# A gated mix of linear attention and an MLP on one core: three groups of products split into 64-row halves, and the blocks' order rewritten

## The chip, the cores and the metric

One core of one Trainium2 chip. The kernel is launched once per run; the time of a run is the device time in microseconds (us). The kernel before was run three times: 446.23, 444.49 and 444.58 us, median 444.58. A profile of one execution on the chip gives the durations of single instructions. TensorE (PE in the profile) multiplies, with a separate instruction that loads the stationary operand (PEld); VectorE is DVE, ScalarE is ACT, GpSimd is POOL, and SyncE (SP) issues most DMAs.

## The reference

```python
x = A_x                                   # 1 x 2048 x 512
g = sigmoid((x * gate_w).sum(-1, keepdims=True))
# A: linear attention, 32 heads of 16
q, k, v = split(x @ wqkv)
phi(u) = concat(softmax(u @ w_phi), softmax(-(u @ w_phi)))
o = phi(q) @ (phi(k).T @ v) / (phi(q) @ phi(k).T @ 1 + 1e-6)
a = o.reshape(B, S, D) @ wo               # wo: 512 x 512
# B: dense, mish, dense
h = x @ w1 + b1                           # w1: 512 x 1376
b = (h * tanh(softplus(h))) @ w2          # w2: 1376 x 512
out = g * a + (1 - g) * b
```

## The kernel before, in words

*Precision.* The large products are done in fp32r, a type of four bytes that TensorE takes in one pass. Each operand X is split into a part h rounded to fp32r and a rest l = X - h, and a product of two operands becomes three: h with h, h with l, l with h.

*Stages.* Stage A goes over the 2048 rows in eight pieces of 256 and makes k, v, q and phi(k); it sums phi(k).T v and phi(k).T 1 in PSUM and SBUF. The change leaves it alone. Stage B goes over four blocks of 512 rows, B0 to B3. A block has eleven hidden groups of 128 (`ORDER`), and for each group i:

- `up` (L516): 12 products of 128 contraction rows into one PSUM bank: w1 (h) with x (h), w1 (l) with x (h), w1 (h) with x (l), four pieces of the contraction each. The bank holds 128 hidden columns of 512 rows.
- `mi` (L527, ScalarE): mish from that bank into SBUF, which frees the bank. `hi` (L532, ScalarE) makes h, `lo` (L540, GpSimd) makes l. Group 0 has an odd number of rows and needs a second `hi` and a part of `lo` on ScalarE; `gr` reads its gate row from the same bank.
- `down` (L559; steps `dn0` to `dn9`, and `df0` to `df3` for the last group): h and l as stationary operands against w2, for four row tiles t: three products each, 12 in all (8 for group 0), summed into four banks, one for each t, over the whole block. `fi` (VectorE) joins a finished bank with the attention part and stores it.

Attention in a block: `nu` (num) multiplies phi(q) by the sums in 64-row, 32-column pieces of the array, `oh` (ScalarE) and `ol` (VectorE) split the result, `wo_` (L676) multiplies by wo in 12 products per row tile, and `ag` (ScalarE) scales it out of its bank. `cd` adds what is left of group 0 in four 32-row pieces. While a block's products run, VectorE and ScalarE make phi(q) of the next one (`mx`, `mn`, `d0`, `d1`, `E`, `S`, `T`, `D`, ..., `es`, `tr`).

*PSUM.* Eight banks: three called "a" (`up`, half of `nu`, `wo`), four called "dn" (the sums of `down`), one called "kv" (`nu`, and `wo` for even t). A bank goes to the next user in turn, once the last one's reader is done.

*Order.* Nothing is planned by a program: the texts `BLOCK0` (B0), `BLOCK1` (B1) and `BLOCK` (B2 and B3; L62 to L84) list the steps, `run` (L201) issues them in that order, and `pin` keeps each engine in the order of issue. A "+" means the next block's step. Every product goes through `mm` (L100), so the profile gives L101 for all of them; ScalarE's steps go through `act` (L121).

Of the kernel before, what the change touches and what calls it, by code (L numbers as in the profile page):

```python
# [59 lines left out]


BLOCK0 = """  # L62
    up0 lq3 mi0 gr hi0 lo0 ldo0 ldo1 S1 rS1 up1 up2 mi1 hi1 lo1 wh0 wl0 d02 d12 T0 D0 m0 de0 rd0 sc0 es0 tr0 mi2 hi2 up3 dn0 hc lo2
    mi3 hi3 lo3 T1 D1 m1 de1 rd1 sc1 es1 tr1 mv0 lq0+ lq1+ mx3 mn3 d03 d13 WH0 dn1
    up4 mi4 hi4 lo4 WH1 WL0 dn2 E2 S2 T2 rS2 D2 m2 de2 rd2 sc2 es2 tr2 up5 mi5 hi5 lo5 WL1 dn3 E3 ge gg up6 mi6 hi6 lo6 dn4
    up7 mi7 hi7 lo7 dn5 S3 T3 rS3 D3 m3 de3 rd3 sc3 es3 tr3 mv1 up8 mi8 hi8 lo8 dn6
    mx0+ mn0+ d00+ d10+ mx1+ mn1+ d01+ d11+ lq2+ lq3+ up9 mi9 hi9 lo9 dn7 E0+ E1+ S0+ T0+ LX0 rS0+ D0+ m0+ de0+ rd0+ sc0+
    up10 mi10 hi10 lo10 dn8 dn9 cd nu0 nu1 oh0 ol0 es0+ tr0+ XH0+ XL0+ S1+ T1+ rS1+ LX1 df0 df1 wo0 ag0 wo1 oh1 ol1 ag1 D1+ fi0
    m1+ de1+ rd1+ sc1+ df2 df3 wo2 ag2 fi1 XH1+ XL1+ es1+ fi2 wo3 ag3 fi3 tr1+ mv0+
"""  # L70
BLOCK1 = """
    up0 mi0 hi0 lo0 gr mx2 mn2 d02 d12 mx3 mn3 d03 d13 up1 mi1 hi1 lo1 lq0+ lq1+ E2 E3 hc S2 T2 rS2 D2 m2 de2 rd2 sc2 es2 tr2
    up2 mi2 hi2 lo2 dn0 S3 T3 rS3 D3 m3 de3 rd3 sc3 es3 tr3 mv1 up3 mi3 hi3 lo3 dn1 up4 mi4 hi4 lo4 dn2
    mx0+ mn0+ d00+ d10+ mx1+ mn1+ d01+ d11+ lq2+ lq3+ up5 mi5 hi5 lo5 dn3 E0+ E1+ ge gg
    S0+ T0+ rS0+ D0+ m0+ de0+ rd0+ sc0+ es0+ tr0+ up6 mi6 hi6 lo6 dn4 up7 mi7 hi7 lo7 dn5 cd nu0 nu1 oh0 ol0 S1+ T1+ rS1+ D1+ LX0 LX1
    m1+ de1+ rd1+ sc1+ es1+ dn6 wo0 ag0 wo1 ag1 oh1 ol1 tr1+ mv0+ dn7 up8 mi8 hi8 lo8 mx2+ mn2+ d02+ d12+ mx3+ mn3+ d03+ d13+
    wo2 ag2 up9 mi9 hi9 lo9 dn8 E2+ E3+ up10 mi10 hi10 lo10 wo3 ag3 XH0+ XL0+ XH1+ XL1+ dn9 df0 fi0 df1 fi1 df2 fi2 df3 fi3
"""
BLOCK = """
    up0 mi0 hi0 lo0 gr lq0+ lq1+ S2 T2 rS2 D2 m2 de2 rd2 sc2 es2 tr2 up1 mi1 hi1 lo1 hc up2 mi2 hi2 lo2 dn0  # L80
    S3 T3 rS3 D3 m3 de3 rd3 sc3 es3 tr3 mv1 up3 mi3 hi3 lo3 dn1 up4 mi4 hi4 lo4 dn2
    mx0+ mn0+ d00+ d10+ mx1+ mn1+ d01+ d11+ lq2+ lq3+ up5 mi5 hi5 lo5 dn3 E0+ E1+ ge gg
    S0+ T0+ rS0+ D0+ m0+ de0+ rd0+ sc0+ up6 mi6 hi6 lo6 dn4 cd nu0 nu1 oh0 ol0 es0+ tr0+ S1+ T1+ rS1+ D1+ LX0 LX1 m1+ de1+ rd1+ sc1+
    es1+ dn5 wo0 ag0 wo1 ag1 oh1 ol1 tr1+ mv0+ dn6 up7 mi7 hi7 lo7 wo2 ag2 mx2+ mn2+ d02+ d12+ mx3+ mn3+ d03+ d13+  # L84
    up8 mi8 hi8 lo8 dn7 E2+ E3+ up9 mi9 hi9 lo9 wo3 ag3 up10 mi10 hi10 lo10 dn8 XH0+ XL0+ XH1+ XL1+ dn9 df0 fi0 df1 fi1 df2 fi2 df3 fi3
"""


@with_exitstack
def tile_gated_mix(ctx: ExitStack, tc: tile.TileContext, xT, wv, wkT, wqT, bd, w1a, w1b, b1, w2a, w2b, wo, out):  # L90
# [6 lines left out]
    pin = tc.keep_in_program_order  # L97
    V, G_, A_, Sy = nc.vector, nc.gpsimd, nc.scalar, nc.sync

    def mm(*a, **k):  # L100
        return pin(nc.tensor.matmul(*a, **k))  # L101
# [410 lines left out]
    def b_ops(b):  # L512
        key = ("B", b)
        U, dn, eTs, num, ohl, io, ed = {}, {}, {}, {}, {}, {}, {}

# [159 lines left out]
        for t in range(4):  # L675
            def wo_(t=t):  # L676
                num["wo", t] = ps = psum("wo", ("kv", "a")[t % 2])
                woh, wol = [kt(wob[x], 512) for x in "hl"]

                todo = [(G, a, w) for G in range(NG) for a, w in ((0, woh), (0, wol), (1, woh))]  # L680
                if t % 2 == 0:
                    todo.sort(key=lambda x: x[1])
                for n, (G, a, w) in enumerate(todo):
                    o = a * 512 + (G % 2) * SC + (t % 2) * P
                    mm(ps, ohl[t // 2, G // 2][:, o : o + P], w[:, G, :], start=(n == 0), stop=(n == 3 * NG - 1))

            def ag(t=t):
                i = 4 * b + t
                io[t] = k2("io", "io")
                act(io[t], num["wo", t], scale=g_sb[:, i : i + 1])  # L690

            def most():

                i = S // P - 1
                pin(V.scalar_tensor_tensor(io[3], dn[3], og_sb[:, i : i + 1], io[3], op0=ALU.mult, op1=ALU.add))

            def rest():

                i = S // P - 1
                for j, eng in enumerate((Sy, A_)):  # L700
                    cs = slice(256 * j, 256 * j + 256)
# [7 lines left out]
                    pin(V.scalar_tensor_tensor(io[3][:, cs], ps, og_sb[:, i : i + 1], io[3][:, cs], op0=ALU.mult, op1=ALU.add))  # L709
# [182 lines left out]
```

## Time and profile before

| | us |
|---|---|
| median of three runs | 444.58 |
| the runs | 444.49 to 446.23 |
| span of the profiled execution (its own time outside the profiler isn't given) | 442.5 |
| TensorE busy | 437.8 |
| VectorE busy | 313.2 |
| ScalarE busy | 201.4 |
| GpSimd busy | 159.6 |
| weight loads busy (under the products) | 359.9 |

How to read it: the span runs from the first to the last instruction of one execution. Products overlap in the array, so one's duration (0.389 us for 512 columns) is longer than the distance from one start to the next; it is the distance that counts. A row of the timeline gives the start, the length, the engine, the line, the tile written and the tiles read, the rows and columns of the array in use (128*128), the shape of the moving operand and the number of instructions that were merged.

### The profile page before, as it was taken

The page shows a single profiled execution, that of the slowest core. Times are in us where ns is not written, and L with a number is a line of the kernel's source. Part 1 is how long each engine was busy: PE and PEld are TensorE (multiplying, and loading weights), DVE is VectorE, ACT ScalarE, POOL GpSimd, SP SyncE. Part 2 cuts the span into 40 slices and gives each one's busy share as a digit, 9 for nine tenths or more (in the row PEclk, how much of TensorE's full clock was granted, in tenths as well). Part 3 has the DMA queues.
Part 4 walks back from the last instruction along what each step waited for, and adds up shares of the span by engine and source line. Part 5 has one row for each costly group of instructions (what it writes and reads, how often), then busy time and mean ns, then how long its engine had stood idle before and what let it go on. Part 6 is the DMA issues. An engine that isn't in the chain of part 4 may idle for free.

```text
span 442.5 us, 7179 instructions
## 1 busy us (share of the span) xinstructions
PE 437.8 (99%) x2874; PEld 359.9 (81%) x2874; DVE 313.2 (71%) x420; ACT 201.4 (46%) x286; POOL 159.6 (36%) x100
## 2 busy tenths in 40 slices
PE   8999999999999999999999999999999999999996
PEld 7888888888888888887888878888878888887885
DVE  3987739559699999999999898279679329601103
ACT  3644523533345455736376533646352645341330
POOL 3078694785662453621024120215310222411121
PEclk9999999999999999999999999999999999999999
DMA  7721631524403136425362533222605302310002
GB/s 265 283 96 48 191 120 50 188 86 133 167 29 116 49 84 209 142 101 168 128 205 96 159 124 120 75 96 95 191 0 192 94 2 96 134 57 1 0 0 96
DMA packets 29001, 49.64 MB, mean 112 GB/s; under 512 B 6308, under 2 KB 15012, under 8 KB 28968
## 3 DMA queue, kind: packets, MB, share of 16 engines
q1 hardware_dynamic: 28648, 48.79, 32.9%
q8 instruction: 22, 0.36, 0.3%
q10 hardware_dynamic: 288, 0.39, 0.3%
q14 instruction: 11, 0.09, 0.1%
q0 software_dynamic: 32, 0.01, 0.0%
HBM read 31.73 MB, written 16.79 MB: 110 GB/s over the span
## 4 chain that ended last, share of the span: by engine, by line
PE 98%; DMA 1%; SPq 0%; DVE 0%; issue 0%
PE proj L101 30%; PE up L101 27%; PE down L101 27%; PE wo L101 10%; PE kvp L101 2%; PE num L101 2%; DMA wT<-in_wkT_dram 1%; PE fuse L101 1%; PE rest L101 0%; DVE io L709 0%; SPq L157 0%; SPq L149 0%
## 5 line engine op out<-in xcount | busy, mean ns | idle before, releaser
L543 POOL TENSOR_TENSOR l<-act,h 128x512 fp32r<-128x512 f32 (+1 forms) x44 | 62.6, 1425 | 215.5 <-ACT h L121 192.7
L121 ACT ACTIVATE act<-up,b1s 128x512 f32<-128x512 f32 x44 | 30.3, 688 | 83.1 <-PE up L101 81.0
L330 POOL TENSOR_TENSOR zacc<-zacc,E 128x1024 f32<-128x1024 f32 x16 | 39.7, 2479 | 39.9 <-DVE E L287 31.4
L121 ACT ACTIVATE E<-E 128x1024 f32<-128x1024 f32 x32 | 33.5, 1060 | 36.0 <-DVE E L272 35.9
L287 DVE TENSOR_TENSOR E<-E,Sm 128x1024 f32<-128x1024 f32 x32 | 45.1, 1409 | 1.0
L101 PE MATMUL wo<-woh,ohl 128*128 128x512 f32 x128 | 41.2, 389 | 0.0
L276 DVE TENSOR_REDUCE Sm<-E 128x64 f32<-128x1024 f32 x32 | 38.5, 1204 | 0.0
L101 PE MATMUL down<-w2ah,h 128*128 128x512 f32 x96 | 37.6, 392 | 0.0
L101 PE MATMUL down<-w2al,h 128*128 128x512 f32 x80 | 31.2, 390 | 0.0
L101 PE MATMUL down<-w2ah,l 128*128 128x512 f32 x80 | 31.1, 389 | 0.0
L121 ACT ACTIVATE h<-act 128x512 fp32r<-128x512 f32 (+2 forms) x48 | 30.3, 632 | 1.6
L101 PE MATMUL down<-w2bh,h 128*128 128x512 f32 x78 | 30.6, 392 | 0.0
L101 PE MATMUL down<-w2bl,h 128*128 128x512 f32 x78 | 30.4, 389 | 0.0
L101 PE MATMUL down<-w2bh,l 128*128 128x512 f32 x78 | 30.4, 389 | 0.0
L431 DVE TENSOR_TENSOR xbl<-xraw,xbh 128x1024 fp32r<-128x1024 f32 x8 | 10.9, 1378 | 27.1 <-ACT xbh L121 27.1
L256 DVE TENSOR_REDUCE mx<-proj 128x32 f32<-128x512 f32 x16 | 11.0, 689 | 25.5 <-PE proj L101 25.5
L101 PEld LDWEIGHTS wo<-woh,ohl 128*128 128x128 f32 x128 | 24.0, 188 | 5.0
L121 ACT ACTIVATE io<-wo,g_sb 128x512 f32<-128x512 f32 x16 | 11.0, 690 | 36.0 <-PE wo L101 34.7
L121 ACT ACT_TABLE_LOAD x19 | 24.4, 1283 | 3.5 <-PE up L101 3.2
L101 PE MATMUL up<-xbh,w1ah 128*128 128x512 f32 x96 | 25.8, 390 | 0.0
L101 PE MATMUL up<-xbh,w1al 128*128 128x512 f32 x96 | 25.7, 389 | 0.0
L101 PE MATMUL up<-xbl,w1ah 128*128 128x512 f32 x96 | 25.7, 389 | 0.0
(125 smaller groups left out, 978.3 us busy)
## 6 DMA issues: line engine op xcount, KB each, us to landing
ed<-E SPq DMA_DIRECT2D x16, 512.0 KB, 2.9
eT<-ed SPq DMA_DIRECT2D x64, 128.0 KB, 3.2
xraw<-in_xT_dram SPq DMA_DIRECT2D x15, 512.0 KB, 4.3
pqd<-qs SPq DMA_DIRECT2D x16, 256.0 KB, 2.1
pq<-pqd SPq DMA_DIRECT2D x16, 256.0 KB, 3.8
out_dram<-io SPq DMA_DIRECT2D x15, 256.0 KB, 2.0
raw<-in_w1a_dram SPq DMA_DIRECT2D x3, 512.0 KB, 4.6
raw<-in_w2a_dram SPq DMA_DIRECT2D x3, 512.0 KB, 3.7
```

The costliest lines, as they stand in the source:

```text
L101: return pin(nc.tensor.matmul(*a, **k))
L121: return pin(A_.activation(out_, in_, fn, **k))
L256: pin(V.tensor_reduce(d[name], hv(src()), axis=AX.X, op=op))
L276: pin(V.tensor_reduce(d["S"], hv(d["E"][:, :]), axis=AX.X, op=ALU.add))
L287: pin(eng.tensor_mul(hv(d["E"][:, :]), hv(d["E"][:, :]), d["S"][:, :, None].to_broadcast([P, 2 * H, DH])))
L330: at(key, f"z{t}", lambda d=d: pin(G_.tensor_add(zacc, zacc, d["E"])))
L431: pin(V.tensor_sub(xb[b][1][:, :, sl], kt(raw[h], SC), f32(xb[b][0][:, :, sl])))
L543: pin(G_.tensor_sub(U[i]["l"][:n, :], U[i]["a"][:n, :], f32(U[i]["h"][:n, :])))
```

## The change

Each product of `up`, `down` and `wo_` is given as two: contraction rows 0 to 63 and 64 to 127, which are different halves of the array. A new function `weave` takes the list of products of several steps and issues them in pairs. The first half goes through the list from its beginning, the second half from its middle and then around, so that the two halves of a pair write to different banks. Both halves of a product add into the same bank at different times. Where a bank goes from one half to the other, an empty instruction on TensorE waits for the last product of the other half in that bank. The steps are named in parentheses in the texts, such as `(up0|up1|up2)`: 36 products, 36 pairs.

The texts are new. `up` goes out in threes, or in twos with a `down`; `wo` in pairs or mixed with `up` and `down`. Steps of the other engines keep their places by and large; `oh1` and `ol1` come directly after `oh0` and `ol0`, and `fi` takes the order 0, 2, 1, 3. In B3 the last two groups' `down` for t = 0 to 2 and the tile `rest` stay whole. The work of the other engines is the same.

```diff
+    def weave(ops):
+        n = len(ops)
+        todo = [(r, ops[(i + r * (n // 2)) % n]) for i in range(n) for r in (0, 1)]
+        banks = [op[0].name for _, op in todo]
+        last = {b: i for i, b in enumerate(banks)}
+        for i, (r, (out_, a, w, opens, closes)) in enumerate(todo):
+            b, s = banks[i], slice(64 * r, 64 * r + 64)
+            row, ins = newest.get(b, (r, None))
+            if row != r:
+                hold = pin(nc.tensor.nop())
+                tc.add_manual_dep(hold.ins, ins, mybir.DependencyInfo(mybir.DependencyClass.Sync, mybir.DependencyReason.DATA), reason="row tiles take turns in a bank")
+            ins = mm(out_, a[s], w[s], start=opens and banks.index(b) == i, stop=closes and last[b] == i, skip_group_check=True)
+            newest[b] = r, ins.ins.name
+
+    newest = {}
...
     def run(text, key, prev=None, nxt=None, prev2=None):
         for w in text.split():
+            if w[0] == "(":
+                weave(sum([ops.pop((key, x))() for x in w[1:-1].split("|")], []))
+                continue
...
-            n = 0
-            for w, a in ((0, xh), (1, xh), (0, xl)):
-                for k in range(KT):
-                    mm(ps, w1_tile(f, w, k), a[:, k, :], start=(n == 0), stop=(n == 3 * KT - 1))
-                    n += 1
             U[i] = {"ps": ps}
+            return [(ps, w1_tile(f, w, k), a[:, k, :], True, True) for w, a in ((0, xh), (1, xh), (0, xl)) for k in range(KT)]
...
-            for n, (a, w) in enumerate(((h, w2_tile(f, 0)), (h, w2_tile(f, 1)), (l, w2_tile(f, 0))) if i else ((h, w2x["a"]), (l, w2x["b"]))):
-                mm(dn[t], a, w, start=(i == 0 and n == 0), stop=(i == (NF - 3 if t == last_t else NF - 1) and n == 2))
+            return [(dn[t], a, w, i == 0, i == (NF - 3 if t == last_t else NF - 1))
+                    for a, w in (((h, w2_tile(f, 0)), (h, w2_tile(f, 1)), (l, w2_tile(f, 0))) if i else ((h, w2x["a"]), (l, w2x["b"])))]
...
+                return [(ps, ohl[t // 2, G // 2][:, o : o + P], w[:, G, :], True, True)
+                        for a, w in ((0, woh), (0, wol), (1, woh)) for G in range(NG) for o in (a * 512 + (G % 2) * SC + (t % 2) * P,)]
```

The new texts (only the first of the old ones is shown):

```diff
 BLOCK0 = """
-    up0 lq3 mi0 gr hi0 lo0 ldo0 ldo1 S1 rS1 up1 up2 mi1 hi1 lo1 wh0 wl0 d02 d12 T0 D0 m0 de0 rd0 sc0 es0 tr0 mi2 hi2 up3 dn0 hc lo2
...
+    (up0|up1|up2) lq3 mi0 gr hi0 lo0 ldo0 ldo1 S1 rS1 mi1 hi1 lo1 wh0 wl0 d02 d12 T0 D0 m0 de0 rd0 sc0 es0 tr0 mi2 hi2 (up3|up4|dn0) hc lo2
+    mi3 hi3 lo3 T1 D1 m1 de1 rd1 sc1 es1 tr1 mv0 lq0+ lq1+ mx3 mn3 d03 d13 WH0 (dn1)
+    mi4 hi4 lo4 WH1 WL0 E2 S2 T2 rS2 D2 m2 de2 rd2 sc2 es2 tr2 (up5|up6|dn2) mi5 hi5 lo5 WL1 E3 ge gg mi6 hi6 lo6 (dn3)
+    (up7|up8|dn4) mi7 hi7 lo7 S3 T3 rS3 D3 m3 de3 rd3 sc3 es3 tr3 mv1 mi8 hi8 lo8 (dn5)
+    mx0+ mn0+ d00+ d10+ mx1+ mn1+ d01+ d11+ lq2+ lq3+ (up9|up10|dn6) mi9 hi9 lo9 E0+ E1+ S0+ T0+ LX0 rS0+ D0+ m0+ de0+ rd0+ sc0+ mi10 hi10 lo10 (dn7)
+    (dn8) cd nu0 nu1 oh0 ol0 oh1 ol1 es0+ tr0+ XH0+ XL0+ S1+ T1+ rS1+ LX1 (dn9) (wo0|wo1|df0) ag0 ag1 D1+ fi0
+    m1+ de1+ rd1+ sc1+ fi1 (wo2|wo3|df2) XH1+ XL1+ es1+ ag2 fi2 ag3 fi3 tr1+ mv0+
 """
 BLOCK1 = """
...
+    (up0|up1|up2) mi0 hi0 lo0 gr mx2 mn2 d02 d12 mx3 mn3 d03 d13 mi1 hi1 lo1 lq0+ lq1+ E2 E3 hc S2 T2 rS2 D2 m2 de2 rd2 sc2 es2 tr2
+    mi2 hi2 lo2 (dn0) S3 T3 rS3 D3 m3 de3 rd3 sc3 es3 tr3 mv1 (up3|up4|dn1) mi3 hi3 lo3 mi4 hi4 lo4
+    mx0+ mn0+ d00+ d10+ mx1+ mn1+ d01+ d11+ lq2+ lq3+ (up5|up6|dn2) mi5 hi5 lo5 E0+ E1+ ge gg
+    S0+ T0+ rS0+ D0+ m0+ de0+ rd0+ sc0+ es0+ tr0+ mi6 hi6 lo6 (dn3) (up7|up8|dn4) mi7 hi7 lo7 mi8 hi8 lo8 cd nu0 nu1 oh0 ol0 oh1 ol1 S1+ T1+ rS1+ D1+ LX0 LX1
+    m1+ de1+ rd1+ sc1+ es1+ (dn5) (wo0|wo1|dn6) ag0 ag1 tr1+ mv0+ mx2+ mn2+ d02+ d12+ mx3+ mn3+ d03+ d13+
+    (wo2|up9|dn7) ag2 mi9 hi9 lo9 E2+ E3+ (wo3|up10|dn8) ag3 mi10 hi10 lo10 XH0+ XL0+ XH1+ XL1+ (dn9) (df0|df2) fi0 fi2 fi1 fi3
 """
 BLOCK = """
...
+    (up0|up1|up2) mi0 hi0 lo0 gr lq0+ lq1+ S2 T2 rS2 D2 m2 de2 rd2 sc2 es2 tr2 mi1 hi1 lo1 hc mi2 hi2 lo2 (dn0)
+    S3 T3 rS3 D3 m3 de3 rd3 sc3 es3 tr3 mv1 (up3|up4|dn1) mi3 hi3 lo3 mi4 hi4 lo4
+    mx0+ mn0+ d00+ d10+ mx1+ mn1+ d01+ d11+ lq2+ lq3+ (up5|up6|dn2) mi5 hi5 lo5 E0+ E1+ ge gg
+    S0+ T0+ rS0+ D0+ m0+ de0+ rd0+ sc0+ mi6 hi6 lo6 (dn3) (dn4) cd nu0 nu1 oh0 ol0 oh1 ol1 es0+ tr0+ S1+ T1+ rS1+ D1+ LX0 LX1 m1+ de1+ rd1+ sc1+
+    es1+ (dn5) (wo0|wo1|dn6) ag0 ag1 tr1+ mv0+ (up7|wo2|up8) mi7 hi7 lo7 ag2 mx2+ mn2+ d02+ d12+ mx3+ mn3+ d03+ d13+
+    mi8 hi8 lo8 (dn7) E2+ E3+ (up9|wo3|up10) mi9 hi9 lo9 ag3 mi10 hi10 lo10 (dn8) XH0+ XL0+ XH1+ XL1+ END
 """
+END = "(dn9) (df0|df2) fi0 fi2 fi1 fi3", "df0 fi0 df1 fi1 df2 fi2 df3 fi3"
```

B2 ends with the first text of `END`, B3 with the second.

More of the change, by code (lines that the diff above doesn't have):

```diff
@@ L62 @@
 BLOCK0 = """
-    up0 lq3 mi0 gr hi0 lo0 ldo0 ldo1 S1 rS1 up1 up2 mi1 hi1 lo1 wh0 wl0 d02 d12 T0 D0 m0 de0 rd0 sc0 es0 tr0 mi2 hi2 up3 dn0 hc lo2
[L64 to L67, printed above, removed]
@@ L68 @@
-    up10 mi10 hi10 lo10 dn8 dn9 cd nu0 nu1 oh0 ol0 es0+ tr0+ XH0+ XL0+ S1+ T1+ rS1+ LX1 df0 df1 wo0 ag0 wo1 oh1 ol1 ag1 D1+ fi0
-    m1+ de1+ rd1+ sc1+ df2 df3 wo2 ag2 fi1 XH1+ XL1+ es1+ fi2 wo3 ag3 fi3 tr1+ mv0+
+    (up0|up1|up2) lq3 mi0 gr hi0 lo0 ldo0 ldo1 S1 rS1 mi1 hi1 lo1 wh0 wl0 d02 d12 T0 D0 m0 de0 rd0 sc0 es0 tr0 mi2 hi2 (up3|up4|dn0) hc lo2
+    mi3 hi3 lo3 T1 D1 m1 de1 rd1 sc1 es1 tr1 mv0 lq0+ lq1+ mx3 mn3 d03 d13 WH0 (dn1)
+    mi4 hi4 lo4 WH1 WL0 E2 S2 T2 rS2 D2 m2 de2 rd2 sc2 es2 tr2 (up5|up6|dn2) mi5 hi5 lo5 WL1 E3 ge gg mi6 hi6 lo6 (dn3)
@@ L70 @@
+    (up7|up8|dn4) mi7 hi7 lo7 S3 T3 rS3 D3 m3 de3 rd3 sc3 es3 tr3 mv1 mi8 hi8 lo8 (dn5)
+    mx0+ mn0+ d00+ d10+ mx1+ mn1+ d01+ d11+ lq2+ lq3+ (up9|up10|dn6) mi9 hi9 lo9 E0+ E1+ S0+ T0+ LX0 rS0+ D0+ m0+ de0+ rd0+ sc0+ mi10 hi10 lo10 (dn7)
+    (dn8) cd nu0 nu1 oh0 ol0 oh1 ol1 es0+ tr0+ XH0+ XL0+ S1+ T1+ rS1+ LX1 (dn9) (wo0|wo1|df0) ag0 ag1 D1+ fi0
+    m1+ de1+ rd1+ sc1+ fi1 (wo2|wo3|df2) XH1+ XL1+ es1+ ag2 fi2 ag3 fi3 tr1+ mv0+
 """
 BLOCK1 = """
-    up0 mi0 hi0 lo0 gr mx2 mn2 d02 d12 mx3 mn3 d03 d13 up1 mi1 hi1 lo1 lq0+ lq1+ E2 E3 hc S2 T2 rS2 D2 m2 de2 rd2 sc2 es2 tr2
@@ L73 @@
[L73 to L77, printed above, removed]
+    (up0|up1|up2) mi0 hi0 lo0 gr mx2 mn2 d02 d12 mx3 mn3 d03 d13 mi1 hi1 lo1 lq0+ lq1+ E2 E3 hc S2 T2 rS2 D2 m2 de2 rd2 sc2 es2 tr2
@@ L78 @@
 """
 BLOCK = """
[L80 to L84, printed above, removed]
@@ L85 @@
-    up8 mi8 hi8 lo8 dn7 E2+ E3+ up9 mi9 hi9 lo9 wo3 ag3 up10 mi10 hi10 lo10 dn8 XH0+ XL0+ XH1+ XL1+ dn9 df0 fi0 df1 fi1 df2 fi2 df3 fi3
+    (up0|up1|up2) mi0 hi0 lo0 gr lq0+ lq1+ S2 T2 rS2 D2 m2 de2 rd2 sc2 es2 tr2 mi1 hi1 lo1 hc mi2 hi2 lo2 (dn0)
+    S3 T3 rS3 D3 m3 de3 rd3 sc3 es3 tr3 mv1 (up3|up4|dn1) mi3 hi3 lo3 mi4 hi4 lo4
+    mx0+ mn0+ d00+ d10+ mx1+ mn1+ d01+ d11+ lq2+ lq3+ (up5|up6|dn2) mi5 hi5 lo5 E0+ E1+ ge gg
+    S0+ T0+ rS0+ D0+ m0+ de0+ rd0+ sc0+ mi6 hi6 lo6 (dn3) (dn4) cd nu0 nu1 oh0 ol0 oh1 ol1 es0+ tr0+ S1+ T1+ rS1+ D1+ LX0 LX1 m1+ de1+ rd1+ sc1+
@@ L199, in at @@
         steps.setdefault((key, name), []).append(fn)
+    ops = {}
     def run(text, key, prev=None, nxt=None, prev2=None):
         for w in text.split():
+            if w[0] == "(":
+                weave(sum([ops.pop((key, x))() for x in w[1:-1].split("|")], []))
+                continue
             k = {"'": prev, '"': prev2, "+": nxt}.get(w[-1], key)
@@ L563, in down, with last_down @@
             h, l = [U[i][x][:, t * P : (t + 1) * P] for x in "hl"]
-            for n, (a, w) in enumerate(((h, w2_tile(f, 0)), (h, w2_tile(f, 1)), (l, w2_tile(f, 0))) if i else ((h, w2x["a"]), (l, w2x["b"]))):
-                mm(dn[t], a, w, start=(i == 0 and n == 0), stop=(i == (NF - 3 if t == last_t else NF - 1) and n == 2))
-        for i in range(NF):
-            at(key, f"up{i}", lambda i=i: up(i))
+            return [(dn[t], a, w, i == 0, i == (NF - 3 if t == last_t else NF - 1))
+                    for a, w in (((h, w2_tile(f, 0)), (h, w2_tile(f, 1)), (l, w2_tile(f, 0))) if i else ((h, w2x["a"]), (l, w2x["b"])))]
+        def last_down(i, t):
+            for n, (o, a, w, _, closes) in enumerate(down(i, t)):
+                mm(o, a, w, start=False, stop=closes and n == 2, skip_group_check=True)
+        for i in range(NF):
+            ops[key, f"up{i}"] = lambda i=i: up(i)
+            if i < NF - (2 if b == NB - 1 else 1):
+                ops[key, f"dn{i}"] = lambda i=i: sum([down(i, t) for t in range(4)], [])
+            elif b < NB - 1:
+                for j in (0, 2):
+                    ops[key, f"df{j}"] = lambda i=i, j=j: down(i, j) + down(i, j + 1)
+            else:
+                for t in range(4):
+                    if t != last_t:
+                        at(key, f"df{t}", lambda i=i, t=t: last_down(i, t))
             at(key, f"mi{i}", lambda i=i: mi(i))
@@ L571, in b_ops @@
             at(key, f"lo{i}", lambda i=i: lo(i))
-            for t in range(4):
-                if t != last_t or i < NF - 2:
-                    at(key, f"dn{i}" if i < NF - (2 if b == NB - 1 else 1) else f"df{t}", lambda i=i, t=t: down(i, t))
         at(key, "hc", hc)
@@ L678, in wo_ @@
                 woh, wol = [kt(wob[x], 512) for x in "hl"]
[L680 to L685, printed above, removed]
+                return [(ps, ohl[t // 2, G // 2][:, o : o + P], w[:, G, :], True, True)
+                        for a, w in ((0, woh), (0, wol), (1, woh)) for G in range(NG) for o in (a * 512 + (G % 2) * SC + (t % 2) * P,)]
             def ag(t=t):
@@ L715, in fi @@
                 pin(Sy.dma_start(out[i * P : (i + 1) * P, :], io[t]))
-            at(key, f"wo{t}", wo_)
+            ops[key, f"wo{t}"] = wo_
             at(key, f"ag{t}", ag)
@@ L829, in tile_gated_mix @@
     for b in range(NB):
-        run((BLOCK0, BLOCK1, BLOCK, BLOCK)[b], ("B", b), ("B", b - 1), ("B", b + 1))
-    assert not steps, list(steps)
+        run((BLOCK0, BLOCK1, BLOCK.replace("END", END[0]), BLOCK.replace("END", END[1]))[b], ("B", b), ("B", b - 1), ("B", b + 1))
+    assert not steps and not ops, (list(steps), list(ops))
 _OUTS = [((S, D), 'float32')]
```

## The prediction

> **What bounds the kernel now.** I read the page first: busy time by engine, then the chain that ended last.
>
> ```profile
> PE 437.8 (99%) x2874; PEld 359.9 (81%) x2874; DVE 313.2 (71%) x420; ACT 201.4 (46%) x286; POOL 159.6 (36%) x100
> PE 98%; DMA 1%; SPq 0%; DVE 0%; issue 0%
> PE proj L101 30%; PE up L101 27%; PE down L101 27%; PE wo L101 10%; PE kvp L101 2%; PE num L101 2%; DMA wT<-in_wkT_dram 1%; PE fuse L101 1%; PE rest L101 0%; DVE io L709 0%; SPq L157 0%; SPq L149 0%
> ```
>
> TensorE is busy for 437.8 of 442.5 us and nothing makes it wait; up, down and wo, which the change touches, hold 64% of the chain. Any wait of TensorE is new time, and only shorter products win any. Next, the busy times of the four row blocks B0 to B3 (columns: stretch, length, then PE, PEld, DVE, ACT, POOL, granted clock):
>
> ```profile
> 149.28:221.82 72.54, 72.54 (x384) 59.21 (x377) 69.42 (x93) 38.49 (x53) 22.05 (x15) 1.00 0.41 132
> 221.82:294.18 72.36, 72.36 (x378) 59.12 (x376) 57.16 (x80) 38.96 (x53) 15.04 (x11) 1.00 0.35 117
> 294.18:366.58 72.40, 72.40 (x377) 59.10 (x376) 49.48 (x71) 33.58 (x48) 16.12 (x11) 1.00 0.31 103
> ```
>
> The clock is granted in full. Each block takes 72.4 us, and in B0 VectorE is busy for 69.4 of it: B0 could not lose more than 3 us whatever TensorE did. Now the pace of one product, from the chain in order of time and from the timeline:
>
> ```profile
> 294.34 8.16 PE up L101 x36
> 205.40 0.39 PE L101 MATMUL down<-w2bh,l 128*128 128x512 f32 x1
> 205.72 0.51 PE L101 MATMUL down<-w2al,hc 32*128 32x512 f32 x4
> 206.16 1.96 PE L101 MATMUL num<-eT,kvb 64*32 64x256 f32 x64
> 207.26 0.85 PE L101 MATMUL num<-eT,kvb 64*32 64x256 f32 x24
> 207.69 0.42 PE L101 MATMUL num<-eT,kvb 64*32 64x256 f32 x8
> L101 PE MATMUL num<-eT,kvb 64*32 64x256 f32 x256 | 7.8, 379 | 0.0
> 208.04 0.50 PE L101 MATMUL down<-w2bh,h 128*128 128x512 f32 x1
> 208.38 0.40 PE L101 MATMUL down<-w2bl,h 128*128 128x512 f32 x1
> 206.16 1.48 PEld L101 LDWEIGHTS num<-eT,kvb 64*32 64x32 f32 x64 [0.25 <-issue]
> 208.04 0.19 PEld L101 LDWEIGHTS down<-w2bh,h 128*128 128x128 f32 x1 [0.41 <-ACT ohl L121]
> 208.15 0.19 PEld L101 LDWEIGHTS down<-w2bl,h 128*128 128x128 f32 x1
> ```
>
> 36 products in 8.16 us are 0.2267 us each, every one with weights of its own. The array is already used in pieces here: "num" runs eight 64-row, 32-column pieces per turn, 64 of them in 1.96 us where one takes 0.38 from start to end. Its last three turns (x24) begin at 207.26, the last of them (x8) at 207.69: 0.43 for two turns, 0.215 each. So pieces do run side by side, and a turn of these costs less than 0.2267.
>
> **The change part by part.** *The halves.* In the new text I count 308 products in a block, 284 in B3 (where the last 18 stay whole): 1208 pairs of halves replace 1208 products. A pair's price isn't in the trace. Its ends are 0.215 (num's turn; 0.213 to 0.217 as the two starts are rounded to 0.01) and 0.2267 (today's product): 14 to 16.5 us won at most, 0 at least; the end above is a rival below. I take 0.2267, because the nearest row is another one: four 32-row pieces of the same type (fp32r) and width (512), in four banks at once, the row with x4. They cost 0.51 where one alone behind a switch of shape costs 0.50 (208.04), so they do run side by side. But they end no sooner than a whole product: from 205.72 to the next shape at 206.16 is 0.44; take off their spread, 0.01, and one weight load in the open, 0.11 (from 208.04 to 208.15, where the next load can start), and 0.32 is left, exactly what the 128-row product at 205.40 takes to the next shape at 205.72. For num, whose last piece starts at 207.69 + 0.42 - 0.38 = 207.73, it is 0.31 after a turn of 0.215: the emptying then takes about 0.09 in all three, and the 512 fp32r columns 0.227, whether 32 or 128 rows are at work. Num differs by its type: its tiles are plain fp32, 256 columns in two passes (the code issues 128, the trace has 256). The 0.013 belongs to the stream, by this reading, and halving the rows doesn't remove it.
>
> The Trainium skill, page "TensorE: Matmul & The Clock Gate", section "Measured speedup vs the span model", gives about 4 ns more for each further tile in the array; by it a pair would cost 0.231 and the sum would be 4.8 us higher. The x4 row agrees for a single turn (0.51 against 0.50), but num's starts are spread by 0.04 in a turn (0.42 less 0.38) and its turns still follow at 0.215, so I charge nothing for it.
>
> *The weight loads* double in number. Two 128-column loads of 0.11 fit under 0.2267 even one after the other; num's 64 loads in 1.48 us run side by side. Charged nothing; the other end is a rival below.
>
> *The holds.* An empty instruction waits wherever a bank goes over to the other half: by the new texts 362 at most. Everything on TensorE stands behind it. What it waits for lies at least three turns back (13 times three, else four or more), and a reader of a product starts 0.49 us after that product started (up's twelfth product starts at 295.99 + 1.07 - 0.39 = 296.67, its reader at 297.16, rows below), that is 2.2 turns. So the hold opens in time, and a wait already served costs nothing today: dn0 at 302.34, which waits for ScalarE and GpSimd, starts 0.23 after the up product before it. Charged 0; if each of the 13 laid a load open, 1.4 us.
>
> *The order.* This is the term that I charge. Three up groups are woven over 36 turns, 36 x 0.2267 = 8.16 us: up0's second half runs in turns 18 to 29, up1 and up2 end with the last turn. Before, up0 was ready 5.4 us ahead of dn0; now six turns, 1.36 us. Rows of B2 (ScalarE and GpSimd behind up0, TensorE beside them), of the group up7, and of B0:
>
> ```profile
> 295.99 1.07 PE L101 MATMUL up<-xbl,w1ah 128*128 128x512 f32 x4
> 301.43 1.07 PE L101 MATMUL up<-xbl,w1ah 128*128 128x512 f32 x4
> 302.34 0.39 PE L101 MATMUL down<-w2ah,h 128*128 128x512 f32 x1
> 297.16 0.69 ACT L121 ACTIVATE act<-up,b1s 128x512 f32<-128x512 f32 x1 [5.63 <-PE up L101]
> 297.88 1.29 ACT L121 ACTIVATE h<-act 96x512 fp32r<-96x512 f32 x2
> 298.65 1.29 POOL L543 TENSOR_TENSOR l<-act,h 96x512 fp32r<-96x512 f32 x1 [9.04 <-ACT h L121]
> 347.81 0.69 ACT L121 ACTIVATE act<-up,b1s 128x512 f32<-128x512 f32 x1 [2.09 <-PE up L101]
> 348.52 0.63 ACT L121 ACTIVATE h<-act 128x512 fp32r<-128x512 f32 x1
> 349.29 1.29 POOL L543 TENSOR_TENSOR l<-act,h 128x512 fp32r<-128x512 f32 x1 [4.15 <-issue]
> 345.02 0.69 ACT L121 ACTIVATE io<-wo,g_sb 128x512 f32<-128x512 f32 x1 [1.31 <-DMA eT<-ed]
> 152.33 0.69 ACT L121 ACTIVATE act<-up,b1s 128x512 f32<-128x512 f32 x1 [2.92 <-PE up L101]
> 155.63 0.69 ACT L121 ACTIVATE act<-up,b1s 128x512 f32<-128x512 f32 x1
> ```
>
> - dn0 in B1, B2, B3, alone behind (up0|up1|up2): up0's last turn starts at 29 x 0.2267 = 6.57, mi0 at 7.06, and l is there 2.78 later (297.16 to 299.94), at 9.84; with the load, 9.95. dn0 needs l in its second turn, at 8.16 + 0.23 = 8.39. Wait 1.56, three times: 4.7 us.
> - dn7 in B2 and B3, alone behind (up7|wo2|up8): mi7 at 7.06, l 2.77 later (347.81 to 350.58) and the load make 9.94; needed in the third turn, 8.61. Wait 1.33, twice: 2.7 us.
> - (up3|up4|dn0) in B0: its first turn writes up4 into up1's bank, free once mi1 has read it. mi0 at 7.06, mi1's end 3.99 later (152.33 to 156.32): 11.05, with the load 11.16, against 8.16: 3.0 us.
> - (wo2|wo3|df2) in B0: wo2 takes wo0's bank. wo0 ends in turn 26 of 30: 5.89 + 0.49 + ag0's 0.69 + 0.11 = 7.18 against 6.80: 0.4 us.
> - Elsewhere the up banks (three) and h, l are ready by the same arithmetic; the nearest is (up5|up6|dn2) in B1, where exps stand ahead of mi3: about 0.1.
>
> Sum 10.9 us. oh1 and ol1 move ahead of the next block's scaling and transposes: VectorE's two ol1 steps then hold back es, tr and the stores on SP's queue behind them, whose readers, num's loads, are due a block later; cover gone, it would be 1.4 us a block. fi0, fi2, fi1, fi3 only change turns. The first wait stands at the start of a block, so h and l of that block are all late by it; nothing else gets tighter.
>
> **Sum.** Span 442.5 + 0 (halves) + 10.9 (waits) = 453.4; what lies around the span is the median's 444.6 - 442.5 = 2.1, and the profiled execution's own time is taken to be the median's. Forecast 455.5 us.
>
> **Rivals.** *A pair costs num's turn, not the product's* (the 0.013 is the changing of weights, and small pieces hide it). For it: num's 0.215, with its weights changed each turn. Against it: the x4 row. At 0.2145, 1208 x 0.0122 = 14.7 us are won; a shorter turn lengthens the waits, since ScalarE and GpSimd keep their pace: dn0 1.65, dn7 1.4, B0 3.6, and two places in B1 to B3 where a bank is freed late come to 1.0, together 12.4. Span 440.2, time 442.3, half a per cent faster; it comes out even with before where a pair costs 0.2165 (1208 x 0.0102 = 12.3). The Trainium skill, the same page, section "Back-to-back issue gap", gives 512 / 2.4 + 2.5 ns, 216 ns, for one product at full clock; the trace has 227 for the whole array, so that rule doesn't hold for these products, and if the halves came to it, 13 us would be won, which is this rival.
>
> *The loads set the pace.* In the last products of the kernel, 256 columns wide, loads are what a product waits for:
>
> ```profile
> 437.82 0.28 PE L101 MATMUL rest<-w2bh,l 128*128 128x256 f32 x1
> 437.94 0.28 PE L101 MATMUL rest<-w2bh,h 128*128 128x256 f32 x1
> 438.06 0.28 PE L101 MATMUL rest<-w2bl,h 128*128 128x256 f32 x1
> ```
>
> 0.12 each. If the halves' loads shared one path, a pair would cost 0.24: 1208 x 0.0133 = 16.1 more, 471.6 us. Against it: num's and the x4 row's loads side by side.
>
> *The halves don't overlap at all*: 1208 x 0.2267 = 274 us more, near 730. The x4 row speaks against it.
>
> **The numbers.** Forecast 0.55, num's pace 0.33, load path 0.09, no overlap 0.03. About half a per cent, 2.2 us, is what a measurement of this kernel can tell from no change. The forecast's own range is 450 to 461 (a few of the waits less, the tight holds and the moved ol1 more); num's pace reaches from 439.5 to 446. The range takes both, 439.5 to 461. Faster takes 0.21 of num's 0.33, same 0.11 of it and a little of the forecast, slower the rest.
>
> **What would show it.** Right: halves in pairs about 0.227 apart; TensorE idle before dn0 (1.6 us) and dn7 (1.3) behind GpSimd's l, and 3 us before up3 in B0 behind ScalarE; 72.4 us and the waits in each block. Wrong: pairs at 0.215, or at 0.24 and loads end to end; no idle before dn0; idle time behind the holds. A granted clock below 1.00 would make all of it void.

## The result, and the profile after

The changed kernel takes 473.13 us (median of 4 runs, 472.94 to 473.94); the kernel before, 444.53 (4 runs, 444.28 to 446.23). The ratio is 1.0642, 95% interval 1.0622 to 1.0663: slower by 28.6 us, where 10.9 were forecast. The sign was right; the time lies outside the range, 439.5 to 461.

The page of the kernel after, its span and busy times:

```profile
span 471.3 us, 9590 instructions
PE 452.1 (96%) x4082; PEld 376.4 (80%) x4082; DVE 314.3 (67%) x420; ACT 199.7 (42%) x286; POOL 156.6 (33%) x100
```

TensorE is busy for 452.1 of 471.3 us: 19.2 us idle, against 4.7 before. It is also busy for 14.3 us more with as many pairs as there were products: 3.3 us of it are a slower clock (below), and the rest lies in the waits, which count in part as busy (from the start at 159.11 below to the next it is 2.66 us, 2.16 of it idle). The four blocks and two short stretches of B0 (stretch, length, then PE, PEld, DVE, ACT, POOL, granted clock) show where:

```profile
149.42:232.14 82.72, 77.38 (x691) 67.64 (x686) 69.20 (x92) 37.77 (x53) 21.84 (x15) 0.96 0.34 111
232.14:313.50 81.36, 76.76 (x686) 62.43 (x684) 57.84 (x80) 38.60 (x54) 15.05 (x11) 1.00 0.34 109
313.50:390.51 77.01, 74.70 (x687) 60.33 (x684) 48.56 (x70) 33.17 (x48) 15.10 (x11) 1.00 0.30 97
390.51:471.30 80.79, 75.20 (x668) 62.65 (x664) 24.84 (x37) 24.69 (x40) 14.15 (x11) 0.99 0.16 53
162.60:166.20 3.60, 3.60 (x20) 2.82 (x18) 3.46 (x5) 2.73 (x7) 3.52 (x3) 0.53 0.27 78
224.20:227.60 3.40, 3.40 (x20) 2.65 (x18) 3.40 (x4) 0.00 (x0) 0.00 (x0) 0.51 0.47 170
```

B0, B1 and B2 grew from 72.5, 72.4 and 72.4 to 82.7, 81.4 and 77.0 us (B3's, which runs to the end of the span, from 75.9 to 80.8). In the two short stretches the clock is halved: 20 half products (ten pairs) fall in each, where 0.2267 us a pair would give some 32 and 30. What TensorE waits for in the blocks, the six largest: in total, times, longest (the waits of the products alone; the loads in front of them wait too, so these are lower bounds):

```profile
PE wo L102 <- ACT io L139: 3.8, 2, 2.5
PE down L102 <- POOL l L562: 2.3, 6, 0.6
PE up L102 <- ACT act L139: 2.2, 1, 2.2
PE up L102 <- DVE ohl L698: 1.9, 2, 1.0
PE num L102 <- ACT act L139: 1.6, 2, 1.4
PE up L102 <- DVE xbl L454: 1.4, 2, 0.7
```

Two of the six lines, GpSimd's l before `down` and ScalarE's act before `up`, are waits that the prediction named. One, wo behind ScalarE's io, had been put at 0.4 us; three had not been named.

The timeline of TensorE at the border between the first two groups of B0, and at dn0 of B2:

```profile
158.24 0.39 PE L102 MATMUL up<-xbh,w1ah 64*128 64x512 f32 x1
158.24 0.39 PE L102 MATMUL up<-xbl,w1ah 64*128 64x512 f32 x1
158.46 0.39 PE L102 MATMUL up<-xbh,w1al 64*128 64x512 f32 x1
158.47 0.39 PE L102 MATMUL up<-xbl,w1ah 64*128 64x512 f32 x1
159.11 0.50 PE L102 MATMUL up<-xbh,w1ah 64*128 64x512 f32 x1
161.77 0.49 PE L102 MATMUL up<-xbh,w1al 64*128 64x512 f32 x1 [2.16 <-ACT act L139]
...
321.97 0.50 PE L102 MATMUL down<-w2ah,h 64*128 64x512 f32 x1
322.62 0.50 PE L102 MATMUL down<-w2ah,h 64*128 64x512 f32 x1 [0.15 <-ACT h L139]
323.37 0.50 PE L102 MATMUL down<-w2x,l 64*128 64x512 f32 x2 [0.25 <-POOL l L562]
```

The two halves of a pair start together and the next pair follows 0.2267 later: of some 1200 distances between pairs in the trace, about 970 lie between 0.225 and 0.228, and all small departures from 0.2267 add up to 0.6 us. A pair costs what a product cost. So all that the change lost, it lost between the groups. I measured each group from its start to the start of the next, less 0.2267 for each turn (and less num's own 2.4 us, which it took before as well):

| place | forecast, us | measured, us |
|---|---|---|
| dn0 in B1, B2, B3 | 4.7 | 5.2 |
| dn7 in B2, B3 | 2.7 | 3.7 |
| (up3, up4, dn0) in B0 | 3.0 | 4.4, of which 1.6 at half clock |
| wo2 in B0 | 0.4 | 4.4, of which 1.7 at half clock |
| wo0 and wo2 in B1 (behind ol0 and ag0), up7 in B2 and B3 (behind ol1) | 0 | 4.5 |
| num in B1 | 0 | 3.1 |
| xl at the start of B0 and B1 | 0 | 2.2 |
| smaller ones, B1 | 0.1 | 1.0 |
| sum | 10.9 | 28.5 |

The spans differ by 28.8. Behind the rows with a forecast of nothing stand two stalls of other engines that the prediction had not looked for. ScalarE and VectorE at oh1 and ol1 in B0 and B1, and what TensorE then waits for:

```profile
220.97 1.08 ACT L139 ACTIVATE ohl<-num 128x512 fp32r<-128x512 f32 x2 [9.29 <-PE wo L102]
221.59 1.29 DVE L698 TENSOR_TENSOR ohl<-num,ohl 128x512 fp32r<-128x512 f32 x2 [8.34 <-ACT ohl L139]
222.88 1.27 ACT L139 ACTIVATE io<-wo,g_sb 128x512 f32<-128x512 f32 x2
223.62 0.72 PE L102 MATMUL wo<-woh,ohl 64*128 64x512 f32 x3 [2.48 <-ACT io L139]
289.26 1.08 ACT L139 ACTIVATE ohl<-num 128x512 fp32r<-128x512 f32 x2 [10.25 <-PE down L102]
289.89 1.29 DVE L698 TENSOR_TENSOR ohl<-num,ohl 128x512 fp32r<-128x512 f32 x2 [8.72 <-ACT ohl L139]
```

and before, the first instruction of oh1 in B0:

```profile
213.86 0.60 ACT L121 ACTIVATE ohl<-num 128x512 fp32r<-128x512 f32 x1 [0.67 <-PE wo L101]
```

`ohl` has two buffers (`k4`: `"oh": 2`), and oh0 fills both, one for each half of the heads. oh1 cannot write before wo0 and wo1 have read them. In the old text oh1 stood behind wo1; in the new one it stands before, at the head of ScalarE's queue, and everything behind it waits: 9.3 us in B0 (0.7 before), 10.3 in B1, with VectorE 8.3 and 8.7 us idle behind it. In B0 and B1 the two ag steps, which free wo's banks, are among what waits.

The second stall, in B1 of the kernel after:

```profile
243.76 0.69 ACT L139 ACTIVATE act<-up,b1s 128x512 f32<-128x512 f32 x1
246.43 2.01 ACT L139 ACTIVATE E<-E 128x1024 f32<-128x1024 f32 x2
247.52 1.22 DVE L299 TENSOR_REDUCE Sm<-E 128x64 f32<-128x1024 f32 x1 [5.51 <-ACT E L139]
267.75 1.06 ACT L139 ACTIVATE E<-E 128x1024 f32<-128x1024 f32 x1 [4.90 <-DVE E L295]
275.93 0.67 ACT L139 ACTIVATE act<-up,b1s 128x512 f32<-128x512 f32 x1
276.65 1.09 PE L102 MATMUL num<-eT,kvb 64*32 64x256 f32 x30 [1.40 <-ACT act L139]
```

and before, the same mi1 and exponential:

```profile
228.10 0.69 ACT L121 ACTIVATE act<-up,b1s 128x512 f32<-128x512 f32 x1
230.77 1.06 ACT L121 ACTIVATE E<-E 128x1024 f32<-128x1024 f32 x1
```

Before, mi1 began 6.3 us into B1 (228.10 - 221.82); now 11.6 (243.76 - 232.14), because up0 and up1 end late. E2 and E3 stand behind mi1 on ScalarE. VectorE waits 5.5 us for them, so all its later steps come late. E0+ and E1+ of the next block stand ahead of mi6, mi7 and mi8 on ScalarE and wait for VectorE (4.9 us). num needs the bank that mi8 reads: 3.1 us. That is a group's late end, seen by TensorE some 33 us later.

### The profile page after: what moved, and what is told of

It is laid out like the page before. It is cut to its first block, busy times and chain, and to the rows that moved or that the text cites. A ratio compares the mean times of both kernels' runs of the same rounds, so it can differ in the third digit from the quotient of the medians.

```text
span 471.3 us, 9590 instructions
## 1 busy us (share of the span) xinstructions
PE 452.1 (96%) x4082; PEld 376.4 (80%) x4082; DVE 314.3 (67%) x420; ACT 199.7 (42%) x286; POOL 156.6 (33%) x100
## 5 line engine op out<-in xcount | busy, mean ns | idle before, releaser
L102 PE MATMUL wo<-woh,ohl 64*128 64x512 f32 x256 | 62.4, 396 | 3.8 <-ACT io L139 3.8
L102 PE MATMUL down<-w2ah,h 64*128 64x512 f32 x192 | 59.3, 396 | 1.0 <-ACT h L139 0.7
L102 PE MATMUL up<-xbh,w1al 64*128 64x512 f32 x192 | 52.9, 392 | 2.2 <-ACT act L139 2.2
L102 PE MATMUL up<-xbl,w1ah 64*128 64x512 f32 x192 | 52.5, 398 | 1.4 <-DVE xbl L454 1.4
L102 PE MATMUL up<-xbh,w1ah 64*128 64x512 f32 x192 | 52.5, 390 | 0.0
L102 PEld LDWEIGHTS wo<-woh,ohl 64*128 64x128 f32 x256 | 44.3, 189 | 10.0 <-ACT io L139 4.6
L102 PE MATMUL down<-w2al,h 64*128 64x512 f32 x160 | 48.9, 387 | 0.0
L102 PE MATMUL down<-w2ah,l 64*128 64x512 f32 x160 | 48.8, 387 | 0.0
L102 PE MATMUL down<-w2bh,h 64*128 64x512 f32 (+1 forms) x150 | 43.9, 394 | 0.3
L102 PE MATMUL up<-xbh,w1bl 64*128 64x512 f32 x160 | 44.1, 387 | 0.0
```

## The experiments

Each ran on the same chip as the kernel before, and its ratio is to the runs of that kernel there. T is the theory that the time is lost in waits which the texts make: groups that end late, and oh1's early place. H is that the halves and their holds cost it. G is that the new sequence of the steps costs it, whatever form the products have.

### oh1 and ol1 back behind ag0

```diff
-... nu0 nu1 oh0 ol0 oh1 ol1 es0+ ... (wo0|wo1|df0) ag0 ag1
+... nu0 nu1 oh0 ol0 es0+ ... (wo0|wo1|df0) ag0 oh1 ol1 ag1
```

and the same in BLOCK1 and BLOCK.

> The changed kernel, with oh1 and ol1 back behind (wo0|wo1|..) and ag0. Theory T: a pair of halves costs what the whole product cost; the 28.6 us that were added are two waits of the new order. One is oh1, which needs the two buffers that oh0 holds until wo1 is through, so that ScalarE and VectorE stand still meanwhile: by the excess of the weaves 2.6 us and 1.7 at half clock in B0, 0.9 + 3.1 + 2.2 in B1, 1.1 in B2 and in B3, 12 to 13 us. T expects 459 to 462 us. Rival H (the halves and their holds cost the time): 470 or more, nothing but the order of two steps is changed.

Measured: 467.94 us (ratio 1.0534, 1.0515 to 1.0553). Early oh1 costs 5.2 us of the 28.6. That lies between what the two theories expected: most of the time is somewhere else. The rows that stay, of this run:

```profile
161.10 0.60 PE L102 MATMUL up<-xbh,w1al 64*128 64x512 f32 x1 [2.16 <-ACT act L139]
242.88 1.22 DVE L299 TENSOR_REDUCE Sm<-E 128x64 f32<-128x1024 f32 x1 [6.54 <-ACT E L139]
272.01 1.09 PE L102 MATMUL num<-eT,kvb 64*32 64x256 f32 x30 [1.39 <-ACT act L139]
```

The bank of up1 in B0, ScalarE's late exponentials in B1 and num behind them are unchanged.

### Whole products in the new texts

`weave` gives each product whole, 128 rows, in the order of the list; no holds.

```diff
-        for i, (r, (out_, a, w, opens, closes)) in enumerate(todo):
...
+        for out_, a, w, opens, closes in ops:
+            b = out_.name
+            left[b] -= 1
+            mm(out_, a, w, start=opens and b not in seen, stop=closes and left[b] == 0, skip_group_check=True)
+            seen.add(b)
```

> The changed kernel's order with whole products, each group one after the other in the list's order; no halves, no holds. T: the other wait is that a group ends late in its weave (dn0 4.8, dn7 3.6, the first turns of B0 about 5 with the half clock); that goes, oh1's stays: 458 to 462 us. Rival H: all of it goes, 445 to 448. Rival G (steps in threes are too coarse, whole or not): 470 or more.

Measured: 449.77 us (1.0122, 1.0097 to 1.0146). T's range was too high by 8 us, H's too low by 1.8: where groups end one after the other, the early oh1 costs little. This run takes the halves and the late ends away together and doesn't decide between the two. The same with oh1 and ol1 late:

> Both undone: whole products in the list's order, oh1 and ol1 back behind wo; left of the change are the threes and the places of down and wo. T: 445 to 449 us. H: the same. G: 457 or more.

Measured: 446.20 us (1.0036, 1.0024 to 1.0048). The new sequence of the steps, and of wo's products in their list, costs 1.5 us. G falls, and the early oh1 with whole products costs 3.6.

### Whole products, each list begun from its middle

Whole products, no halves, no holds, oh1 late. Of three groups the first and the second end in the turns in which they end in the change (29 and 35, counted from 0), and the middle of the list is needed at once, as there; the third ends in turn 17, where its other half ends in turn 35 in the change.

```diff
-        for out_, a, w, opens, closes in ops:
+        for out_, a, w, opens, closes in ops[len(ops) // 2 :] + ops[: len(ops) // 2]:
```

> As e3, but each weave's whole products begin in the middle of the list, as the second halves do: up0 ends in turn 29 of 36 as in the woven kernel, and up1 in the last. No halves, no holds. T (what counts is when a group ends): as e1, 456 to 461 us, with TensorE idle 1.6 us before dn0 in B1 to B3. H: as e3, 445 to 449.

Measured: 462.32 us (1.0397, 1.0382 to 1.0413), a little above T's range and far from H's. 16.1 us come back without a single half-row product. So the order inside each lot, with groups that end late and a middle that is needed early, is shown to be the main cost. With halves put in place (the first experiment) it is 5.6 more. By the traces it lies in two places mainly: num of B0 starts 3.5 us later than in this run (208.70 against 205.24), num of B1 as much (268.09 against 264.61), num of B2 5.1 (342.44 against 337.35), and then little more. In B0 it is the border of the first two groups: the halves open the banks of up3 and up4 in one turn, so both must be free (a gap of 2.66 us, then half clock), where whole products open one bank after the other and stand for 0.3 us there: 4 of the 5.6 us. In B1 num waits longer; whether the halves make that or the third group's later end is not shown.

### The second half two thirds ahead

The changed kernel with oh1 late, and another distance between the halves where three groups end in an `up`: the first group then ends in turn 24 instead of 30.

```diff
-        todo = [(r, ops[(i + r * (n // 2)) % n]) for i in range(n) for r in (0, 1)]
+        off = 2 * n // 3 if n == 36 and ops[-1][0].name[:2] == "up" else n // 2
+        todo = [(r, ops[(i + r * off) % n]) for i in range(n) for r in (0, 1)]
```

> The changed kernel with oh1, ol1 late (467.9 us), and in the weaves of three groups that end in an up group (up0 up1 up2 in each block, and up7 wo2 up8, up9 wo3 up10 in B2 and B3) the second half 24 turns ahead instead of 18, so that the first group ends in turn 24 instead of 30, 1.36 us earlier, and the low part of x is needed 1.36 us later. Theory T, most of what is left is the late end of the woven groups: the waits before dn0 (three of 1.6), dn7 (two of 1.4) and on xl in B0 shrink or go, and up4's bank in B0 comes free 1 to 2 us earlier, so that no stretch at half clock follows: 7 to 11 us less, 457 to 461. Rival H, what is left lies in the halves and their holds: still 36 turns, the same holds or more of them: 465 to 470.

Measured: 462.70 us (1.0407, 1.0391 to 1.0422), 5.2 less. It is below H's range and above T's by 1.7. By place: up4's bank in B0 4.2 to 1.5, with no stretch at half clock there; xl in B0 1.5 to 0.4; dn0 in B1 1.8 to 0.7; dn7 1.5 to 0.6, twice. Against that, dn5 behind num in B1 lost 1.4 where it was 0.2: a stretch at half clock lies there now, from 0.7 us behind the end of a wait of 1.39 (columns as for the blocks above):

```profile
268.40:271.80 3.40, 3.40 (x28) 2.27 (x16) 3.33 (x5) 1.60 (x3) 0.01 (x1) 0.50 0.00 0
```

And dn0 in B2 and B3 stayed at 1.5, although up0 ended 1.36 earlier. The reason, in B2 (VectorE, GpSimd, TensorE):

```profile
312.33 1.23 DVE L311 TENSOR_TENSOR E<-E,Sm 128x1024 f32<-128x1024 f32 x1
312.50 2.19 POOL L563 TENSOR_TENSOR l<-act,h 96x512 fp32r<-96x512 f32 x1 [9.99 <-ACT h L140]
314.75 0.50 PE L102 MATMUL down<-w2x,l 64*128 64x512 f32 x2 [0.74 <-POOL l L563]
```

GpSimd's l takes 2.19 us here, against 1.27 in the kernel after: the earlier start falls on VectorE's product E. What was won at up0 is lost in l. And each of these weaves now has two places where a bank goes to the other half in the very next turn; the pairs there are 0.325 apart, 0.10 for each hold that is not served in time.

### oh1 early, alone, in the kernel before

```diff
-... oh0 ol0 es0+ tr0+ XH0+ XL0+ S1+ T1+ rS1+ LX1 df0 df1 wo0 ag0 wo1 oh1 ol1 ag1
+... oh0 ol0 oh1 ol1 es0+ tr0+ XH0+ XL0+ S1+ T1+ rS1+ LX1 df0 df1 wo0 ag0 wo1 ag1
```

and the same in BLOCK1 and BLOCK.

> The kernel before with one part of the change alone: oh1, ol1 directly behind ol0 in the text of every block, ahead of ag0 and of the next block's scaling. Theory T, the early place alone makes ScalarE and VectorE stand until wo0 and wo1 have read the two oh buffers; with wo's groups in list order (wo0 ends first) TensorE feels only a part: 2 to 6 us slower in all, 446.5 to 450.5, most of it in B0 and B1. Rival, the early place costs what the changed kernel lost by it (5.2 us or more): 450 or above. Rival as the prediction had it, charged nothing: 444 to 445.5.

Measured: 450.39 us (1.0120, 1.0096 to 1.0144), 5.8 us slower, at the upper end of T and at the lower end of the rival that has it cost what it cost in the changed kernel (5.2); the prediction's zero falls. Rows of its timeline, of the chain in order of time, and of the windows:

```profile
214.74 0.69 DVE L669 TENSOR_TENSOR ohl<-num,ohl 128x512 fp32r<-128x512 f32 x1 [5.16 <-ACT ohl L121]
225.31 1.06 ACT L121 ACTIVATE xbh<-xraw 128x1024 fp32r<-128x1024 f32 x1 [3.92 <-DMA xraw<-in_xT_dram]
226.42 1.19 PE L101 MATMUL up<-xbh,w1ah 128*128 128x512 f32 x4 [3.04 <-ACT xbh L121]
```

```profile
220.34 4.95 DMA xraw<-in_xT_dram
```

```profile
229.80:233.20 3.40, 3.40 (x14) 2.66 (x13) 3.40 (x5) 2.36 (x4) 0.96 (x1) 0.77 0.76 290
```

VectorE stands 5.2 us before ol1. Behind it stands XL0+, which frees the buffer of the next x; the DMA that fills it goes out at 220.3 instead of 212.9, so the h part of x for B1 is late and TensorE waits 3.0 us at the border of the blocks. Eight products at half clock follow (1.6 us). TensorE's wait is at other steps than in the changed kernel; the stall of ScalarE and VectorE at oh1 that leads to it is the same.

### The exponentials of B1 first

The changed kernel with oh1 late, and E2 and E3 ahead of mi0 in B1.

```diff
-    (up0|up1|up2) mi0 hi0 lo0 gr mx2 mn2 d02 d12 mx3 mn3 d03 d13 mi1 hi1 lo1 lq0+ lq1+ E2 E3 hc
+    (up0|up1|up2) mx2 mn2 d02 d12 mx3 mn3 d03 d13 E2 E3 mi0 hi0 lo0 gr mi1 hi1 lo1 lq0+ lq1+ hc
```

> The changed kernel with oh1, ol1 late (467.9 us), and in the text of B1 alone the next features (mx2 to d13) and their exponentials E2, E3 moved ahead of mi0, so that ScalarE does them before it turns to the late up0 and up1. Theory T, in B1 num waits 3.1 us (2.5 of it in the distances between its products) because E2 and E3 stand behind mi1, which comes 5.3 us later in the block than before, so VectorE stands idle 6.5 us and E0+, E1+ and mi7, mi8 are late by it: that idle time and num's wait in B1 go (num's surplus below 0.5 us, VectorE's wait for E below 1), while mi0 comes 3 us later and dn0 in B1 waits 3 us more, perhaps with a stretch at half clock behind it: 464 to 471 in all. Rival, num's wait comes from up8's own late end or from the holds: num still waits 2.5 us or more, and dn0's 3 us come on top: 471 or above.

Measured: 469.27 us (1.0557, 1.0540 to 1.0575). num's surplus in B1 is gone (5.5 to 2.4 us with cd, their own time), and VectorE no longer waits for E there; dn0 in B1 went from 1.8 to 6.0, a stretch at half clock included, and wo behind num from 1.1 to 0.4. So the chain from up1's late end to num is shown. The time is not won, only moved: ScalarE has to do both, and both are needed early.

### Trains of one shape

The kernel before with nine trains of 40 products at its end.

```diff
+    def train(kind, n, cols, rows, dt=F32R):
...
+        ps = [psum(kind, "dn") for _ in range(q)]
+        for i in range(n):
+            for j in range(q):
+                r = slice(rows * j, rows * j + rows)
+                mm(ps[j][:, :cols], wt[r], xt[r, :cols], start=True, stop=True, skip_group_check=True)
```

> The kernel before with nine trains of 40 products behind its end, each train of one shape: whole products of fp32r with 512, 384 and 256 columns, 64-row halves side by side in two banks with 512, 384 and 256 columns, four 32-row quarters with 512, and plain fp32 of 256 columns, whole and in halves. If the surplus of a product over 512/2.4 ns belongs to the stream (17 parts in 16), 384 columns take 0.170 us; if it is a fixed part of each product, 0.173. If the loads of two halves run beside each other, a pair of 256-column halves takes what a whole product takes, 0.12 or less; if they share one path, about 0.24.

The trains in the timeline (start, length of the whole train):

```profile
439.15 9.26 PE L101 MATMUL pa<-xbh,w1bh 128*128 128x512 f32 x40
448.25 7.12 PE L101 MATMUL pb<-xbh,w1bh 128*128 128x384 f32 x40
455.21 4.95 PE L101 MATMUL pc<-xbh,w1bh 128*128 128x256 f32 x40
460.08 9.36 PE L101 MATMUL pd<-xbh,w1bh 64*128 64x512 f32 x80
469.28 7.12 PE L101 MATMUL pe<-xbh,w1bh 64*128 64x384 f32 x80
476.24 4.95 PE L101 MATMUL pf<-xbh,w1bh 64*128 64x256 f32 x80
481.12 9.51 PE L101 MATMUL pg<-xbh,w1bh 32*128 32x512 f32 x160
490.56 17.53 PE L101 MATMUL ph<-xbh,w1bh 128*128 128x256 f32 x80
508.02 17.54 PE L101 MATMUL pi<-xbh,w1bh 64*128 64x256 f32 x160
```

This kernel ran once, in 528.16 us; only its trains are read. From one start to the next, over 40: whole products of 512, 384 and 256 columns take 0.2275, 0.174 and 0.122 us; pairs of halves 0.230, 0.174 and 0.122; four quarters 0.236; a plain fp32 pass of 256 columns 0.218, whole or in halves (17.53 and 17.54 us for the trains). From 384 to 512 columns it is 0.0535 us, 0.418 ns a column, which is 1/2.4; at 512 and at 384 columns 0.014 is left over. So the 0.013 is a fixed part of each fp32r product, not a share of the stream, and halves carry it as whole products do. The loads of two halves run side by side: 256-column pairs take 0.122, not 0.24.

## Why the prediction was wrong

*What bounds the kernel* held. Any wait of TensorE is new time, and that, with the slower clock behind two of the waits, is all that happened.

*The halves* held: a pair takes 0.2267. The reading behind it, that the 0.013 belongs to the stream, fell; the trains show a fixed part, which halving does not remove either. The distinction by type held: plain fp32 takes 0.218 for its pass at any split. The Trainium skill, page "TensorE: Matmul & The Clock Gate", section "Back-to-back issue gap", has N / 2.4 + 2.5 ns; the slope is what the trains show, the constant is 14 ns for fp32r here and about 5 for fp32 (0.218 less 512/2.4). So the rival with num's pace falls for fp32r, as the two with dearer pairs do by the 0.2267.

*The weight loads and the holds* held: nothing. The two-thirds run shows what a hold costs where it isn't served in time, 0.10 (the bound was 0.11 each).

*The order* is the step that failed, and in three ways. The named waits were there and nearly right: dn0 4.7 against 5.2, dn7 2.7 against 3.7, B0 3.0 against 4.4; for the first two, h was late as well as l, and an open load in front of each of them was not counted.

First, "Elsewhere the up banks (three) and h, l are ready by the same arithmetic" was wrong. It followed each late group only to its first reader on TensorE. It didn't follow ScalarE's queue: mi1 5.3 us later in the block pushes E2 and E3, these push VectorE, and that comes back at num (3.1 us). Nor did it look at the low part of x, which the list's middle needs in turn 2 instead of turn 8: 1.1 us in B0, and 1.1 in B1 that go when oh1 is put back. The run begun from the middle, 16.1 us with whole products, prices the late ends and early needs together, the named waits included but for the one in B0.

Second, oh1's new place was put at nothing in the sum, with 1.4 us a block should cover go. The text counted the buffers of PSUM and not those of `ohl`. Moved ahead of its buffer's readers, the step stalls two engines for 8 to 10 us; that is 5.2 us of the end, 5.8 in the kernel before, 3.6 with whole products in the new texts.

Third, the clock. The text had the granted clock below 1.00 only as something that would make it void. It fell behind the two longest waits, both in B0: 1.6 and 1.7 us. In no run here did it fall in the blocks without a wait of TensorE just before, so these 3.3 us are counted with the waits.

In all, from the medians, each step on top of the last: new sequence 1.5, order inside the lots 16.1, halves 5.6 (4 of it where two banks open at once in B0, with the half clock behind that), early oh1 5.2; 28.4 of 28.6.

No version here beats the kernel before. Pairs cost what products cost, TensorE was 99% busy, and the new sequence with whole products and oh1 late, 446.2 us, is no faster.

## What to carry to other kernels

Interleaving two or three groups doesn't only mix them: it moves the end of each towards the end of the lot. Follow that through every in-order queue that a reader stands in, and around again to the bottleneck, before charging a wait. When a step is moved ahead, check every buffer that it writes for readers that still stand behind it: in an in-order queue one such step holds up all the rest. Splitting a full product over the rows of the array won nothing here: 512 columns took 0.227 to 0.230 us with 128 rows or with two times 64.

## What the runs showed of the hardware that was not expected

*Half clock behind short waits.* In five of the runs the granted clock falls to a half in the blocks, for 3.41 us each time, with products 0.42 to 0.43 apart instead of 0.2267. That begins 0.3 to 1.5 us after TensorE has started again from a wait. The idle time of that wait was 2.16 and 2.48 us in the kernel after, 2.16 with oh1 put back, 3.04 in the kernel before with oh1 early, 2.16 and 3.12 with the exponentials first, and 1.39 in the two-thirds run. Waits of 1.92 (whole products, oh1 early), of 1.40 (num in the kernel after, and in the run begun from the middle) and of 1.19 (two-thirds run, B0) had none behind them. So the length of the wait alone does not decide. The Trainium skill, page "TensorE: Matmul & The Clock Gate", section "Part 1: The HAM clock gate", says that the clock is halved after an idle window of about 3.4 us, and that the windows run freely. The length agrees with the trace; that seven waits shorter than such a window were enough does not agree with it as it stands.

*GpSimd beside VectorE.* l on 96 rows took 1.27 us in the kernel after and up to 2.2 when it met VectorE's product of two tiles. In the row above l ends 1.13 us after VectorE's product does (314.69 against 313.56), about l's own length. The Trainium skill, page "SBUF — State Buffer", section "SBUF: two separate sides", says that the two engines share a pair of ports, which one of them holds for a whole instruction. This trace agrees.

*Quarters* cost a little: 0.236 for four, 0.230 for a pair and 0.2275 for a whole product, each in trains of 40.
